# The order in which the PSUM banks go to the products behind the attention

## The chip, the cores and the metric

The kernel runs on one core of a Trainium2 chip. The metric is the device time of one execution in microseconds (us). TensorE (PE, with its weight loads as PEld) multiplies into PSUM, eight banks of 512 float32 values for each of 128 partitions; VectorE (DVE) and ScalarE (ACT) read and write PSUM and the on-chip memory SBUF; GpSimd (POOL) works on SBUF alone; SyncE (SP) issues most of the transfers. Each engine works through its own queue in order and waits on semaphores for the others.

## The reference

An attention over 2 batches of 12 heads (448 positions, 64 dimensions) is followed by two layers on its 896 x 768 output. The change concerns the first product of the first layer, h = x @ w_in.

```python
scores = scale * np.matmul(q, k.transpose(0, 1, 3, 2))        # causal mask, softmax -> attn
attn_out = np.matmul(attn, v)
x = attn_out.transpose(0, 2, 1, 3).reshape(B * S, H * D)      # 896 x 768

h = x @ w_in                                                  # 768 x 2048
g = np.where(h >= 1, h, np.where(h <= -1, 0.0, (h + 1) ** 2 / 4.0))
x = g @ w_out                                                 # 2048 x 768

gate, val = x @ w_gate, x @ w_val                             # 768 x 1536 each
out = (gate * (1.0 / (1.0 + np.exp(-gate))) * val) @ w_out2   # 1536 x 768
```

## The kernel before

Every product of the layers is made in three matmuls: each operand is split into a high part (what float32r keeps) and a low rest, and high x high, high x low and low x high are summed in PSUM (`mm3`, L85 to L88). x is kept transposed, in two groups g of 448 token columns: group 0 is the first half of the positions of both batches, group 1 the second half. h is made in 16 slices f of 128 rows; a product of a slice and a group is 6 x 3 = 18 matmuls of 128 x 448 into one bank (`h_products`, L267). Its squashing leaves the bank by several steps on DVE and ACT.

The attention runs first, group 0 and then group 1, as a software pipeline whose order is written out in `ORDER`. It holds seven of the eight banks: two score tiles of two banks (`ps_s`), one of two banks for the transposes (`ps_t`), one for the values (`ps_o`). One bank is left, the pool `mm_a` (L310). While group 1's attention runs, this bank takes the h products of group 0, slices 0 to 8, one after the other (`filler`, L488). Each is read by `h_relu` (L282) and `h_max` (L287, L288), and with L288 the bank is free for the next; `g_hi` and `g_lo` (L293, L297) then work on a copy in SBUF.

After the attention its seven banks go to a new pool `mm_b` (L564). The products that follow are group 1's slices 0 to 8 and then both groups' slices 9 to 15 (`h_chunk`, L567). Here a bank is read and written by five steps: L575 (DVE), L576 (ACT, on the clipped copy), L578 (DVE, back into the bank), L293 (ACT) and L297 (DVE); only then is it free. Between these steps `W.tick` puts the preparation of the weights to come: three operations of `narrow` on DVE (L99, L102, L105), a cast on ACT (L195) and a subtraction on POOL (L196).

Which bank a product gets is decided by `bank()` (L262): it takes the first pool of the list `banks`, puts it at the end and asks it for a tile. During the attention the list holds `mm_a` alone. A tile waits until the last user of its bank is done. A scheduler then arranges the instructions of each engine by the times that it estimates, so that products written one after the other can change places or interleave; in the order printed below, a number behind a tile's name tells tiles apart. Tiles 1748 and 1821 are the eighth and the ninth product in `mm_a`, 1860 the first and 1890 the second product of `h_chunk`.

Of the kernel before, what the change touches and what calls it, by code (L numbers as in the profile page):

```python
# [63 lines left out]
def fused_kernel(ctx: ExitStack, tc: tile.TileContext, qk, v, w_in, w_out, w_gv, w_o2, out):  # L64
# [195 lines left out]
    banks = []  # L260
# [301 lines left out]

    gt1 = gctx.enter_context(tc.tile_pool(name="gt1", bufs=1))
    mm_b = ctx.enter_context(tc.tile_pool(name="mm_b", bufs=7, space=PSUM))  # L564
    banks += [mm_b] * 7

    def h_chunk(g, f, gt):  # L567
        for ps in h_products(g, f):
# [246 lines left out]
```

## Time and profile before

| | |
|---|---|
| median of 3 runs | 603.63 us (603.3 to 603.74) |
| the profiled execution | 603.42 us |
| its span, first to last instruction | 601.6 us |
| TensorE busy | 593.4 us, 99% |
| VectorE busy | 441.5 us, 73% |
| ScalarE busy | 232.4 us, 39% |
| GpSimd busy | 117.1 us, 19% |

The profile page and the trace are of one execution; 603.42 - 601.6 = 1.8 us of its time lie outside the span. A busy time is an average over the whole program, so the stretches are read apart: the attention with its fillers up to about 146 us, the rest of h up to about 230 us, and then the second product of the first layer and the second layer. A matmul's row lasts longer than the distance to the next matmul's start, since matmuls are pipelined: what one costs in a row of them is the distance from start to start.

### The profile page before, as it was taken

How to read it: one execution, taken by the hardware profiler on the slowest of the kernel's cores; microseconds unless marked ns; L12 is line 12 of the kernel's file. 1: busy time of each engine (PE TensorE's matmuls, PEld its weight loads, DVE VectorE, ACT ScalarE, POOL GpSimd, SP SyncE). 2: the span in 40 equal slices, each digit the busy share in tenths (PEclk: the TensorE clock that was granted, in tenths of full speed). 3: DMA queues.
4: the chain of work that ended last, by engine and by line, in shares of the span. 5: the costliest groups of instructions: out<-in, count | busy, mean ns of one | idle time of the engine just before them, and what ended most of it. 6: DMA issues, size and time to landing. Idle time of an engine off the chain costs nothing.

```text
span 601.6 us, 8762 instructions
## 1 busy us (share of the span) xinstructions
PE 593.4 (99%) x3334; PEld 521.3 (87%) x3334; DVE 441.5 (73%) x811; ACT 232.4 (39%) x499; POOL 117.1 (19%) x68
## 2 busy tenths in 40 slices
PE   9999999999999999999999999999999999999997
PEld 5766667668999999999999999999999999999997
DVE  3999999872886777666874699489787899863401
ACT  3987777653344433111121454224224342512100
POOL 0000000000311221323133212124122233632300
PEclk9999999999999999999999999999999999999999
DMA  8575554300151234567644303133333333544002
GB/s 260 175 212 171 172 176 151 106 1 1 53 158 33 84 93 150 182 210 245 194 133 146 106 1 105 53 105 106 103 111 103 105 106 115 200 157 145 1 1 92
DMA packets 23417, 72.52 MB, mean 121 GB/s; under 512 B 2640, under 2 KB 9616, under 8 KB 23376
## 3 DMA queue, kind: packets, MB, share of 16 engines
q1 hardware_dynamic: 20784, 69.61, 36.7%
q10 hardware_dynamic: 2592, 2.36, 1.1%
q8 instruction: 26, 0.43, 0.3%
q14 instruction: 15, 0.12, 0.1%
HBM read 66.85 MB, written 5.11 MB: 120 GB/s over the span
## 4 chain that ended last, share of the span: by engine, by line
PE 84%; DVE 13%; ACT 1%; DMA 1%; issue 0%; ACTq 0%
PE mm L81 34%; PE mm L660 27%; PE mm L749 5%; PE mm L751 5%; PE mm L750 5%; DVE s L368 3%; DVE p L406 2%; PE mm L83 2%; PE s L81 1%; DVE wt L105 1%; DVE wt L102 1%; PE mm L473 1%; ACT p L382 1%; DVE wl L196 1%; DMA wraw<-w_in 1%; PE t L83 1%
## 5 line engine op out<-in xcount | busy, mean ns | idle before, releaser
L196 POOL TENSOR_TENSOR wl<-wt,wh 128x768 fp32r<-128x768 f32 (+1 forms) x52 | 102.5, 1976 | 428.3 <-ACT wh L195 428.3
L195 ACT CAST wh<-wt 128x768 fp32r<-128x768 f32 (+1 forms) x61 | 49.7, 816 | 152.0 <-DVE wt L105 40.7
L99 DVE TENSOR_SCALAR wt<-wraw 128x768 int32<-128x768 int32 (+1 forms) x64 | 44.9, 701 | 41.8 <-POOL wl L196 36.7
L102 DVE SCALAR_TENSOR_TENSOR wt<-wraw,wt 128x768 int32<-128x768 int32 (+1 forms) x64 | 72.5, 1132 | 0.8
L81 PE MATMUL mm<-gh,wh 128*128 128x448 f32 x192 | 70.1, 365 | 0.0
L81 PE MATMUL mm<-gh,wl 128*128 128x448 f32 x192 | 70.1, 365 | 0.0
L81 PE MATMUL mm<-gl,wh 128*128 128x448 f32 x192 | 70.1, 365 | 0.0
L660 PE MATMUL mm<-yl,wh 128*128 128x448 f32 x180 | 65.7, 365 | 0.0
L660 PE MATMUL mm<-yh,wl 128*128 128x448 f32 x180 | 65.7, 365 | 0.0
L660 PE MATMUL mm<-yh,wh 128*128 128x448 f32 x180 | 65.7, 365 | 0.0
L105 DVE SCALAR_TENSOR_TENSOR wt<-wraw,wt 128x768 int32<-128x768 int32 (+1 forms) x64 | 64.4, 1007 | 0.7
L81 PE MATMUL mm<-xh,wh 128*128 128x448 f32 x165 | 62.6, 379 | 2.4 <-DVE q L288 2.4
L749 PE MATMUL mm<-wh,uh 128*128 128x384 f32 x168 | 56.1, 334 | 0.0
L750 PE MATMUL mm<-wl,uh 128*128 128x384 f32 x168 | 56.1, 334 | 0.0
L751 PE MATMUL mm<-wh,ul 128*128 128x384 f32 x168 | 56.1, 334 | 0.0
L382 ACT ACTIVATE p<-s,mx 112x112 f32<-112x112 f32 (+3 forms) x96 | 46.4, 497 | 20.0 <-DVE mx L370 14.4
L81 PE MATMUL mm<-xl,wh 128*128 128x448 f32 x138 | 50.4, 365 | 0.0
L81 PE MATMUL mm<-xh,wl 128*128 128x448 f32 x138 | 50.2, 365 | 0.0
L368 DVE TENSOR_REDUCE s<-s 112x2 f32<-112x224 f32 (+3 forms) x48 | 35.4, 743 | 6.9 <-PE s L83 6.7
L81 PEld LDWEIGHTS mm<-gl,wh 128*128 128x128 f32 x192 | 36.1, 188 | 2.9
L81 PEld LDWEIGHTS mm<-gh,wl 128*128 128x128 f32 x192 | 36.1, 188 | 2.9
L81 PEld LDWEIGHTS mm<-gh,wh 128*128 128x128 f32 x192 | 36.1, 188 | 2.8
(132 smaller groups left out, 1216.8 us busy)
## 6 DMA issues: line engine op xcount, KB each, us to landing
wraw<-w_gv SPq DMA_DIRECT2D x18, 768.0 KB, 4.3
wraw<-w_in SPq DMA_DIRECT2D x16, 768.0 KB, 4.7
wraw<-w_out SPq DMA_DIRECT2D x12, 768.0 KB, 4.6
wraw<-w_o SPq DMA_DIRECT2D x12, 768.0 KB, 4.2
araw<-w_gv SPq DMA_DIRECT2D x18, 256.0 KB, 4.8
qk_t<-qk SPq DMA_DIRECT2D x12, 336.0 KB, 3.2
wraw<-w_out SPq DMA_DIRECT2D x6, 512.0 KB, 3.8
qk_t<-qk SPq DMA_DIRECT2D x12, 224.0 KB, 3.9
```

The source lines that it names most:

```text
L81: return product(*args, **kw)
L99: yield nc.vector.tensor_scalar(out=t, in0=w[:, :, 1], scalar1=3, scalar2=0x3FFFFFF8, op0=ALU.logical_shift_left, op1=ALU.bitwise_and,)
L102: yield nc.vector.scalar_tensor_tensor(out=t, in0=w[:, :, 1], scalar=-0x40000000, in1=t, op0=ALU.bitwise_and, op1=ALU.bitwise_or,)
L105: yield nc.vector.scalar_tensor_tensor(out=t, in0=w[:, :, 0], scalar=29, in1=t, op0=ALU.logical_shift_right, op1=ALU.bitwise_or,)
L195: nc.scalar.copy(out=wh[:, :n], in_=t)
L196: (nc.vector if i < LOW_V else nc.gpsimd).tensor_tensor(out=wl[:, :n], in0=t, in1=wh[:, :n].bitcast(F32), op=ALU.subtract,)
L368: nc.vector.tensor_reduce(out=mx[:, i], in_=s[:C, :, off:off + w], axis=AX.X, op=ALU.max)
L382: nc.scalar.activation(out=p[:, h, off:off + w], in_=s[:C, h, off:off + w], func=AF.Exp, bias=mx[:, i, h:h + 1], scale=0.125, accum_out=sm ...
L660: nc.tensor.matmul(out=ps[:, :N], lhsT=w[a][:, sl], rhs=rows[c][b], start=(first and c == i == 0), stop=(last and c == i == 2), skip_group ...
L749: nc.tensor.matmul(out=ps, lhsT=c, rhs=a, start=(f == 0), stop=False)
L750: nc.tensor.matmul(out=ps, lhsT=c, rhs=b, start=False, stop=False)
L751: nc.tensor.matmul(out=ps, lhsT=d, rhs=a, start=False, stop=(f == FC2 - 1))
```

## The change

The seven banks of `mm_b` are put in front of `mm_a` in the list, and no longer behind it.

```diff
     gt1 = gctx.enter_context(tc.tile_pool(name="gt1", bufs=1))
     mm_b = ctx.enter_context(tc.tile_pool(name="mm_b", bufs=7, space=PSUM))
-    banks += [mm_b] * 7
+    banks[:0] = [mm_b] * 7
```

Before, the first product of `h_chunk` gets the bank `mm_a`, the second to eighth get the banks of `mm_b`, and the ninth `mm_a` again. Now the first to seventh get the banks of `mm_b` and the eighth gets `mm_a`. The circle of eight banks stays the same for all that follows.

TensorE (PE) where the attention's last h product ends, before:

```order
L83 MATMUL mm_1821<-xh_74,wl_1702 128x448
L81 MATMUL mm_1890<-xh_76,wh_764 128x448 [waits DVE_49]
L81 MATMUL mm_1890<-xl_77,wh_764 128x448
...
L81 MATMUL mm_1860<-xh_76,wh_468 128x448 [waits DVE_49]
L81 MATMUL mm_1860<-xl_77,wh_468 128x448
...
L81 MATMUL mm_1860<-xh_76,wl_469 128x448
L81 MATMUL mm_1890<-xh_76,wl_765 128x448
```

The same place on TensorE after the change:

```order
L83 MATMUL mm_1821<-xh_74,wl_1702 128x448
L81 MATMUL mm_1860<-xh_76,wh_468 128x448 [waits DVE_49]
L81 MATMUL mm_1860<-xl_77,wh_468 128x448
...
L81 MATMUL mm_1860<-xh_76,wl_469 128x448
L81 MATMUL mm_1890<-xh_76,wh_764 128x448
L81 MATMUL mm_1890<-xl_77,wh_764 128x448
```

Before, 11 of the second product's 18 matmuls stand ahead of the first product and 7 behind it; now the two products stand one after the other, and the second has no wait of its own. Nothing else on PE moves.

VectorE (DVE) behind the attention's last h product, before (`gl1_0` and `gl1_1` are the low parts of the first and second product's result, `wt_2010` the twelfth weight, which L99 to L105 narrow):

```order
L575 TENSOR_SCALAR m_1879<-mm_1860 128x448 [waits PE_49]
L578 TENSOR_TENSOR mm_1860<-mm_1860,m_1879 128x448 [waits Activation_49]
L575 TENSOR_SCALAR m_1909<-mm_1890 128x448 [waits PE_49]
L99 TENSOR_SCALAR wt_2010<-wraw_1913 128x768 [waits DMAHW3_49,Pool_49]
L297 TENSOR_TENSOR gl1_0_1886<-mm_1860,gh1_0_1885 128x448 [waits DMAHW6_49,DMAHW4_49,DMAHW7_49,DMAHW1_49,Activation_49]
L578 TENSOR_TENSOR mm_1890<-mm_1890,m_1909 128x448 [waits Activation_49]
L102 SCALAR_TENSOR_TENSOR wt_2010<-wraw_1913,wt_2010 128x768 [waits DVE_49]
L297 TENSOR_TENSOR gl1_1_1917<-mm_1890,gh1_1_1916 128x448 [waits Activation_49]
```

The same place on VectorE after the change:

```order
L575 TENSOR_SCALAR m_1879<-mm_1860 128x448 [waits PE_49]
L578 TENSOR_TENSOR mm_1860<-mm_1860,m_1879 128x448 [waits Activation_49]
L99 TENSOR_SCALAR wt_2010<-wraw_1913 128x768 [waits DMAHW3_49,Pool_49]
L102 SCALAR_TENSOR_TENSOR wt_2010<-wraw_1913,wt_2010 128x768 [waits DVE_49]
L297 TENSOR_TENSOR gl1_0_1886<-mm_1860,gh1_0_1885 128x448 [waits DMAHW6_49,DMAHW4_49,DMAHW7_49,DMAHW1_49,Activation_49]
L575 TENSOR_SCALAR m_1909<-mm_1890 128x448 [waits PE_49]
L105 SCALAR_TENSOR_TENSOR wt_2010<-wraw_1913,wt_2010 128x768 [waits DVE_49]
L578 TENSOR_TENSOR mm_1890<-mm_1890,m_1909 128x448 [waits Activation_49]
```

The narrowing of the twelfth weight, L99 and L102, now stands ahead of the first step on the second product. Some 25 rows of DVE and nine of ACT change places in this way over the next five products; behind them the order is as before, and POOL and SP have the same instructions in the same order throughout.

## Rows read from the trace of the kernel before

**Rows 1.** The page: busy us, share of the span, instructions.

```profile
PE 593.4 (99%) x3334; PEld 521.3 (87%) x3334; DVE 441.5 (73%) x811; ACT 232.4 (39%) x499; POOL 117.1 (19%) x68
```

**Rows 2.** Busy time by stretch; columns in the first row.

```profile
core 0: us, PE busy (x) PEld busy (x) DVE busy (x) ACT busy (x) POOL busy (x), PEclk, DMA share, GB/s
0.00:141.90 141.90, 137.18 (x1013) 92.59 (x1013) 120.62 (x345) 98.18 (x279) 0.94 (x7) 1.00 0.49 151
141.90:598.19 456.29, 456.25 (x2322) 428.68 (x2322) 320.30 (x467) 134.19 (x221) 116.14 (x61) 1.00 0.35 112
598.19:601.60 3.41, 0.00 (x0) 0.00 (x0) 0.55 (x1) 0.00 (x0) 0.00 (x0) 1.00 0.15 58
```

**Rows 3.** Waits of PE, whole span; PEld, 138 to 200: total us, times, longest.

```profile
PE mm L81 <- DVE q L288: 2.4, 4, 1.3
PE mm L473 <- DVE half_b L478: 1.2, 1, 1.2
PE o L81 <- ACT pt L426: 0.9, 1, 0.9
PE s L81 <- ACT p L382: 0.2, 1, 0.2
...
PEld mm L81 <- DVE q L288: 1.0, 2, 0.8
```

**Rows 4.** Chain of waits around the ninth product's start: start us, us, what.

```profile
139.89 0.64 ACT r L282
...
140.56 0.64 DVE q L287
...
141.22 0.64 DVE q L288
...
141.90 0.47 PE mm L81
```

**Rows 5.** Timeline at the handover: start us, us, engine, line, operation, [idle before].

```profile
145.44 0.37 PE L83 MATMUL mm<-xh,wl 128*128 128x448 f32 x1
145.65 0.36 PE L81 MATMUL mm<-xh,wh 128*128 128x448 f32 x1
...
147.24 0.62 DVE L288 TENSOR_TENSOR q<-mm,q 128x448 f32<-128x448 f32 x1
...
147.68 0.36 PE L81 MATMUL mm<-xl,wh 128*128 128x448 f32 x1
...
147.92 0.19 PEld L81 LDWEIGHTS mm<-xh,wh 128*128 128x128 f32 x1 [0.26 <-DVE q L288]
147.92 0.47 PE L81 MATMUL mm<-xh,wh 128*128 128x448 f32 x1
...
148.23 0.37 PE L81 MATMUL mm<-xl,wh 128*128 128x448 f32 x1
```

**Rows 6.** Busy time of an undisturbed stretch, columns as in rows 2.

```profile
151.88:184.91 33.03, 33.03 (x164) 30.61 (x163) 28.77 (x40) 13.97 (x23) 7.35 (x4) 1.00 0.31 96
```

**Rows 7.** Timelines of POOL, DVE and PE behind the handover.

```profile
152.59 3.65 POOL L196 TENSOR_TENSOR wl<-wt,wh 128x768 fp32r<-128x768 f32 x2 [151.05 <-ACT wh L195]
...
154.48 2.18 DVE L99 TENSOR_SCALAR wt<-wraw 128x768 int32<-128x768 int32 x1
156.58 0.61 DVE L297 TENSOR_TENSOR gl<-mm,gh 128x448 fp32r<-128x448 f32 x1
...
157.65 0.94 DVE L102 SCALAR_TENSOR_TENSOR wt<-wraw,wt 128x768 int32<-128x768 int32 x1
...
161.00 0.55 DVE L99 TENSOR_SCALAR wt<-wraw 128x768 int32<-128x768 int32 x1
...
174.98 0.37 PE L81 MATMUL mm<-xh,wh 128*128 128x448 f32 x1
```

**Rows 8.** Groups by line, 142 to 199 us: count, busy us, mean ns, idle before.

```profile
L102 DVE SCALAR_TENSOR_TENSOR wt<-wraw,wt 128x768 int32<-128x768 int32 x6 | 8.1, 1348 | 0.1
...
L99 DVE TENSOR_SCALAR wt<-wraw 128x768 int32<-128x768 int32 x6 | 5.0, 826 | 1.6 <-POOL wl L196 1.5
```

## The prediction

> **What bounds the kernel now.** I read the page's busy times first. TensorE is busy 593.4 us of a span of 601.6 [rows 1], so the kernel is already almost one row of matmuls, and the question is only in which stretches it is not. The table by stretches answers that [rows 2]. Up to 141.90 us TensorE is busy 137.18 us of 141.90; from there to 598.19 us it is busy 456.25 of 456.29; then follows a tail of 3.41 us in which it does nothing. The granted clock is 1.00 in all three, which is the 2.4 GHz level, so no stretch is slow for that reason. The change takes effect where the attention hands over to the remaining h products, at about 145.65 us, so it falls into the middle stretch, where TensorE has 0.04 us of idle time in 456. Nothing can be taken out there but the work itself, or a bubble that the busy time hides because the row of the matmul ahead reaches into it.
>
> The list of TensorE's waits names the candidate: line 81 waited for the DVE operation q of line 288, 2.4 us in 4 waits, the longest 1.3 us [rows 3]. That is the attention's one bank: each h product must wait until L288 has read the product before it for the last time. It would be a mistake to book the 2.4 us to this change. The chain of waits shows where the last of them lies [rows 4]: the eighth product's matmuls end, then come L282, L287 and L288, and the ninth starts at 141.90 us. It belongs to the attention's own nine products, which the change leaves on the one bank; the wait at the handover is not among the four. It shows only in the list of the weight loads (PEld): 1.0 us in 2 waits, 0.8 of it the one at 141.90 [rows 3], which leaves 0.2 to 0.3 for the other.
>
> What the handover itself costs is seen in order of time [rows 5]. The ninth product's last matmul starts at 145.44; the next row starts at 145.65, one pitch later, without a wait, and by the order of the instructions it belongs to tile 1890 in the first of the seven new banks. The old bank becomes free when L288 ends, at 147.24 + 0.62 = 147.86 us. In between TensorE runs 11 matmuls of tile 1890, the last starting at 147.68, and the first on the old bank (tile 1860) starts at 147.92. So the scheduler has already put useful work under the wait, and what is left is the difference between 2.27 us (145.65 to 147.92) and 11 pitches.
>
> **The change part by part.**
>
> Pitch. In an undisturbed piece 164 matmuls start within 33.03 us, counting the first and the last [rows 6]; that is 33.03 / 163 = 0.2026 us from start to start.
>
> The bubble. From 147.68 to 148.23 there are two pitches, 0.405 us undisturbed, but 0.55 us in the rows [rows 5]. The bubble is 0.145 us. Its first piece is 147.68 to 147.92, 0.24 instead of 0.20: a gap of 0.04. The rest is 147.92 to 148.23, 0.31 instead of 0.20: the weights of the waiting matmul start loading at 147.92 together with it, where in other rows they load while the matmul before them runs. With the change, tile 1860 stands in the bank that tile 1890 had, which is free at 145.65 (the row of tile 1890 shows no wait there); tile 1890 takes the second new bank. Both old users of these banks, the attention's scores, ended long before; the last x_lo of the attention, on which every product of group 1 depends, is done too, since tile 1890 needs it too and did not wait. The old bank comes to the eighth product after the handover, 7 products of 18 matmuls later (25.5 us after 145.65), when it has been free for over 20 us. **Gain: 0.145 us.** The lower bound is 0, if the late load is paid again where the two products now meet; the upper bound is the bubble itself, since TensorE has no other idle time near. I take the upper end, since the nearest row of two products that meet on free banks, 145.44 to 145.65, goes on at the pitch.
>
> On the load the Trainium skill can be set against the row. In the page "TensorE: Matmul & The Clock Gate", section "Step-by-step: what each phase is for", it says that TensorE pulls a weight load ahead of matmuls in flight when it goes to the background weight buffer. By that the weights of the waiting matmul would have been in place before 147.92, only the 0.04 us would be bubble, and the sum would come to 603.38 us; the row, where the load starts only at 147.92, after 0.26 us of idle time, speaks for the 0.145.
>
> What moves on the other engines. On PE 11 matmuls move behind 18; none is added or removed. The first product of group 1 is therefore complete 11 matmuls (2.2 us) earlier and the second at the same place as before. DVE and ACT take up the first product's five steps (L575, L576, L578, L293, L297) earlier; on DVE the narrowing of the next weight (L99, L102) now stands ahead of L575 of the second product. Both queues are in order, so if L99 waits for GpSimd, all that stands behind it waits: L297 of the first product and the whole chain of the second. L99 did not wait here before, but it was slow: 2.18 us at 154.48, beside a GpSimd row that runs from 152.59 for 3.65 us, against 0.55 us at 161.00 [rows 7]. Such a stretch is worth 1.6 us, on DVE. Its cover is the bank turn: the first product's bank was released at 156.58 + 0.61 = 157.19 us and is asked for again by the product that starts at 174.98 us [rows 7], so 17.8 us are free. From 142 to 199 us six L102 had a mean of 1.35 us against 0.94 for one that ran beside no GpSimd row, and six L99 had 0.83 against 0.55 [rows 7, 8]: 6 x 0.41 + 6 x 0.28 = 4.1 us of stretching in all. Even doubled it does not use up 17.8 us. **Cost: 0**, under that cover.
>
> The weights. The slot that the tenth weight is cast into (L195) comes free when the first product of group 1 has been through, some 2 us earlier than now; it was not late before, since none of TensorE's waits is for a weight [rows 3]. Nothing is gained. SP and POOL issue the same instructions in the same order, so no transfer moves past another.
>
> The rotation. There are eight banks in the same circle before and after, only entered one place later, so every later tile follows the last user of its bank by eight tiles as before. The tail is untouched: TensorE ends at 598.19 us [rows 2], and the last copy and the output transfer follow.
>
> Sum against the profiled execution: 603.42 - 0.145 = 603.28 us. That execution lies 0.21 us below the median of the three runs, 603.63; from the median the same step gives 603.49. I put the forecast between, at **603.4 us**. The gain is 0.02%, a tenth of the 0.2% (1.2 us) that a measurement of this kernel can tell from no change, and less than the 0.44 us between the three runs.
>
> **Rivals.**
>
> A: the whole wait comes back as gain. If the handover had cost what the old bank's wait lasts, 2.27 us, the time would be 603.42 - 2.27 = 601.15 us, faster by 0.4%. For it speaks that the wait is real: L282, L287 and L288 take 1.9 us after the ninth product. Against it speak the 11 matmuls in the rows between 145.65 and 147.68; they are work that must be done anyway, and after the change it is done later. Chance 0.02.
>
> B: the reordered DVE queue makes TensorE wait (slower). The place is the ninth product after the handover, at 174.98 us, the first that reuses a bank: if DVE hangs on L99 behind GpSimd so long that the first product's bank is not released by then, TensorE stands until the release has run. The nearest row for such a stand is the attention's own, from L282 at 139.89 to the ninth product at 141.90 [rows 4]: 2.01 us, which gives 603.28 + 2.01 = 605.3 us, slower by 0.3%. It decides from a delay of 17.8 us on. For it speaks that the order moves L99 and L102 forward, and that they collide with GpSimd; against it, that the stretch of the whole window is 4.1 us. Chance 0.03.
>
> C: the bubble stays. If the change only swaps which product pays for a late weight load, the time is 603.42 us from the profiled run and 603.63 from the median. For it speaks that two products still meet at 145.65 and at 149.3; against it, the pitch from 145.44 to 145.65. Chance 0.12, on the same side of every bound as the forecast.
>
> **How the numbers follow.** Forecast 0.83, A 0.02, B 0.03, C 0.12. Faster by over 0.2% needs A: 0.02. Slower by over 0.2% needs B: 0.03. Within 0.2%: 0.95. For the range the unknown costs give hardly any width, 603.28 to 603.63. What remains is the run itself: the stretch up to 141.90 us, with its waits for transfers and its queues on DVE, is where runs can differ, and three runs spread over 0.44 us. I allow twice that on either side, 602.5 to 604.3 us.
>
> **What would show it.** In the profile of the changed kernel: the weight loads' waits for q of L288 fall from two to the one at 141.90, while TensorE's own four stay; from 145.65 on all matmuls start 0.20 us apart, with none that is 0.47 us long; the first product's 18th matmul starts near 145.65 + 17 x 0.2026 = 149.1 us, and L575 follows at once; and the stretch from the ninth product's start to TensorE's end shrinks from 456.29 us by 0.1 to 0.2. The prediction is wrong if a gap on PE appears near 175 us (B), if TensorE waits for a weight between 178 and 210 us, or if that stretch shrinks by more than 0.5 us (A).

## The result: 610.9 us, 1.2% slower

The changed kernel takes 610.91 us (median of 4 runs, 610.19 to 611.10) against 603.68 us of the kernel before in the same measurement (4 runs, 603.30 to 603.85). The ratio is 1.0119, its 95% interval 1.0101 to 1.0136. The forecast was 603.4, no change. The time lies outside the range, on the side that had a chance of 0.03, and the mechanism given for that side is not what happened.

First the busy times of the profile after, one row for all engines (compare [rows 1]), and the two stretches in which TensorE works, with the columns of [rows 2]:

```profile
PE 600.1 (99%) x3334; PEld 521.1 (86%) x3334; DVE 434.7 (71%) x811; ACT 232.7 (38%) x499; POOL 114.6 (19%) x68
```

```profile
0.00:141.57 141.57, 136.79 (x1012) 92.54 (x1012) 120.56 (x345) 98.02 (x279) 0.94 (x7) 1.00 0.48 151
141.57:604.98 463.41, 463.35 (x2322) 428.53 (x2322) 313.58 (x467) 134.65 (x221) 113.68 (x61) 1.00 0.34 110
```

The span grew from 601.6 to 608.4 us, and TensorE's busy time grew by as much with it: 600.1 instead of 593.4 us for the same 3,334 matmuls. The stretch up to the ninth product is 0.33 us shorter, the tail behind it takes 3.42 us (3.41 before), and the stretch between them went from 456.29 to 463.41 us: 7.12 us, with 0.06 us of idle time and a granted clock of 1.00, the 2.4 GHz level, as before. Nothing waits longer. The list of TensorE's waits, and that of the weight loads from 138 to 200 us (total us, times, longest), against [rows 3]:

```profile
PE mm L81 <- DVE q L288: 2.3, 4, 1.3
...
PEld mm L81 <- DVE q L288: 0.8, 1, 0.8
```

The second wait of the weight loads, that of the handover, is gone. The timeline of TensorE at the handover shows the same, against [rows 5]:

```profile
145.39 0.37 PE L81 MATMUL mm<-xh,wh 128*128 128x448 f32 x1
...
147.87 0.37 PE L81 MATMUL mm<-xh,wh 128*128 128x448 f32 x1
148.07 0.37 PE L81 MATMUL mm<-xl,wh 128*128 128x448 f32 x1
```

The row runs through without the matmul of 0.47 us. So the change does what it was meant to do, and the loss is in no gap. It is seen in the count of matmuls in a stretch of 100 us; columns as in [rows 2]. First 200 to 300 us after the change, then the same of the kernel before:

```profile
200.00:300.00 100.00, 100.00 (x486) 90.81 (x485) 69.21 (x123) 24.87 (x40) 23.99 (x14) 1.00 0.52 167
```

```profile
200.00:300.00 100.00, 100.00 (x495) 92.67 (x494) 71.62 (x123) 24.70 (x41) 24.13 (x14) 1.00 0.52 168
```

There are 486 matmuls where there were 495, in a stretch without any idle time: every matmul costs 1.9% more. Where this begins and ends is seen in the chain of waits after the change (start us, us, what):

```profile
141.57 0.47 PE mm L81
142.04 1.03 PE mm L83 x5
...
145.55 204.60 PE mm L81 x990
...
517.55 0.18 PE mm L749
```

990 matmuls in 204.60 us are 206.67 ns from start to start, where [rows 6] gave 202.6. It holds from the ninth product on (1.03 us for five matmuls, where before it was 1.01) to 517.55 us, where the last stage begins, whose matmuls have 384 columns (L749). The kernel before begins that stage at 510.76 us. From the ninth product's start it takes 375.98 us to get there, before 368.86: all of the 7.12 us. The last stage takes 87.43 us in both (517.55 to 604.98, 510.76 to 598.19). 375.98 us at 206.67 ns are 1,819 matmuls; 1,819 x 4.0 ns = 7.28 us, less the bubble that went.

So 448-column matmuls have two steady paces, 202.67 and 206.67 ns from start to start. What sets them was the question for the chip. Single executions of one and the same kernel fall into two groups, near 603.6 and near 610.6 us; a run below that has no trace is counted as fast or slow by its time.

### The profile page after: what moved, and what is told of

The parts are those of the page before. It is cut to its first block, busy times and chain, and to the rows that moved or that the text cites. A ratio compares the mean times of both kernels' runs of the same rounds, so it can differ in the third digit from the quotient of the medians.

```text
span 608.4 us, 8761 instructions
## 1 busy us (share of the span) xinstructions
PE 600.1 (99%) x3334; PEld 521.1 (86%) x3334; DVE 434.7 (71%) x811; ACT 232.7 (38%) x499; POOL 114.6 (19%) x68
## 4 chain that ended last, share of the span: by engine, by line
PE 83%; DVE 13%; DMA 2%; ACT 1%; issue 0%; SPq 0%; ACTq 0%
PE mm L81 34%; PE mm L660 28%; PE mm L750 5%; PE mm L751 5%; PE mm L749 5%; DVE s L368 3%; DVE p L406 2%; PE mm L83 2%; DVE wt L105 1%; PE s L81 1%; DVE wt L102 1%; ACT p L382 1%; DVE wl L196 1%; DMA wraw<-w_in 1%; PE t L83 1%; PE s L83 1%
## 5 line engine op out<-in xcount | busy, mean ns | idle before, releaser
L196 POOL TENSOR_TENSOR wl<-wt,wh 128x768 fp32r<-128x768 f32 (+1 forms) x52 | 100.3, 1931 | 436.2 <-ACT wh L195 436.2
L99 DVE TENSOR_SCALAR wt<-wraw 128x768 int32<-128x768 int32 (+1 forms) x64 | 40.1, 627 | 47.9 <-POOL wl L196 46.4
L81 PE MATMUL mm<-gh,wh 128*128 128x448 f32 x192 | 70.7, 368 | 0.0
L81 PE MATMUL mm<-gl,wh 128*128 128x448 f32 x192 | 70.7, 368 | 0.0
L81 PE MATMUL mm<-gh,wl 128*128 128x448 f32 x192 | 70.7, 368 | 0.0
L102 DVE SCALAR_TENSOR_TENSOR wt<-wraw,wt 128x768 int32<-128x768 int32 (+1 forms) x64 | 68.5, 1071 | 0.9
L105 DVE SCALAR_TENSOR_TENSOR wt<-wraw,wt 128x768 int32<-128x768 int32 (+1 forms) x64 | 65.2, 1019 | 0.7
L81 PE MATMUL mm<-xh,wh 128*128 128x448 f32 x165 | 62.9, 381 | 2.3 <-DVE q L288 2.3
L749 PE MATMUL mm<-wh,uh 128*128 128x384 f32 x168 | 56.1, 334 | 0.0
L81 PE MATMUL mm<-xl,wh 128*128 128x448 f32 x138 | 50.8, 368 | 0.0
L81 PE MATMUL mm<-xh,wl 128*128 128x448 f32 x138 | 50.8, 368 | 0.0
L81 PEld LDWEIGHTS mm<-gh,wh 128*128 128x128 f32 x192 | 36.0, 188 | 3.7
L81 PEld LDWEIGHTS mm<-gl,wh 128*128 128x128 f32 x192 | 36.0, 188 | 3.6
L81 PEld LDWEIGHTS mm<-gh,wl 128*128 128x128 f32 x192 | 36.0, 188 | 3.6
```

Source lines behind the costliest of these rows:

```text
L81: return product(*args, **kw)
L99: yield nc.vector.tensor_scalar(out=t, in0=w[:, :, 1], scalar1=3, scalar2=0x3FFFFFF8, op0=ALU.logical_shift_left, op1=ALU.bitwise_and,)
L102: yield nc.vector.scalar_tensor_tensor(out=t, in0=w[:, :, 1], scalar=-0x40000000, in1=t, op0=ALU.bitwise_and, op1=ALU.bitwise_or,)
L105: yield nc.vector.scalar_tensor_tensor(out=t, in0=w[:, :, 0], scalar=29, in1=t, op0=ALU.logical_shift_right, op1=ALU.bitwise_or,)
L196: (nc.vector if i < LOW_V else nc.gpsimd).tensor_tensor(out=wl[:, :n], in0=t, in1=wh[:, :n].bitcast(F32), op=ALU.subtract,)
L749: nc.tensor.matmul(out=ps, lhsT=c, rhs=a, start=(f == 0), stop=False)
```

## Experiments

The letters in the expectations stand for these theories. P: the pace is taken where a row of matmuls starts anew, and kept until something interrupts the row. L: it differs from execution to execution of one program. B: the bank that the products get, or their order, sets it. V: an old bank that comes early in the circle protects against the slow pace. Three more came later: D, each new start is a draw whose odds hang on its timing; W and W2, the width of the matmuls ahead of a row sets its pace. In the two runs on the handover's restart, W has another meaning: the short wait sets the pace anew.

**The same two kernels again.** No edit.

> The changed kernel once more. Its trace has no new wait; every 448-column matmul from the ninth product on starts 206.7 ns after the one ahead, where the kernel before has 202.7 on average, over about 1,780 matmuls (4.0 ns x 1,780 = 7.1 us). Theory P (pace): a row of matmuls takes one of two steady paces, fixed by how the row starts after an idle gap, and keeps it until the next gap; the changed kernel has no gap after the ninth product's start. If the start falls the same way every time: 610 to 611 us in every run, 206.7 ns in the trace. Theory L (lottery): each run draws anew, so single runs lie either near 603.5 or near 611. Theory B (bank): the place of the products in the banks sets the pace; 610 to 611 us in every run as well.

> The kernel before once more, for its trace. Theory P (pace drawn where a row of matmuls starts): the ninth product may have either pace (202.7 or 206.7 ns), but from the restart at the handover, the matmul that waits some 0.04 us for the old bank, the pace is 202.7 ns, since all runs of this kernel so far lie between 602.5 and 604.9 us. If the ninth product's pace simply carried through the handover, a ninth product at 206.7 ns would give 206.7 ns behind it and 611 us.

The changed kernel gave 603.41, 603.73 and 603.86 in three runs and 610.17 to 611.57 in seven. The profile is of the run of 603.73: first a stretch with the columns of [rows 2], then the chain.

```profile
200.00:300.00 100.00, 100.00 (x495) 92.68 (x495) 70.91 (x123) 25.54 (x41) 25.54 (x15) 1.00 0.53 173
```

```profile
142.36 0.47 PE mm L81
142.83 1.01 PE mm L83 x5
...
511.07 0.18 PE mm L749
```

The same program, the fast pace from the ninth product on: the pace is not fixed by the instructions (L). With this B falls too, as far as it gives a program one pace. From the ninth product to the 384-column stage it takes 368.71 us, against 368.86 before: 0.15 us less. That is the gain of 0.145 us that the prediction worked out, visible as soon as the pace is the same. The kernel before gave 603.54 here. In the comparisons with the other kernels it ran 81 times; 80 of these runs lie between 602.56 and 605.54 us and one at 610.98. Going by its time, that one run was at the slow pace: the kernel before can fall into it too, but hardly ever does. The changed kernel did so in 11 of 14 runs.

**The old bank second.** Against the changed kernel:

```diff
-    banks[:0] = [mm_b] * 7
+    banks[:] = [mm_b] + banks + [mm_b] * 6
```

> The old bank is handed out second: the first product behind the attention takes the first new bank, the second takes the old one, which is free by then. The instructions stand in exactly the changed kernel's order and there is no gap at the handover. Theory P: as the changed kernel, 610 to 611 us, pace 206.7 ns (or, with another draw at the ninth product's start, 603.5). Theory B: only six of the first eight products are where the changed kernel has them, so a pace of its own for some products, 604 to 610 us. If the gap at the handover were what costs time, 603.3.

603.20 and 603.76 in two runs, 609.72 to 612.74 in eight; ratio to the kernel before 1.0105, 1.0078 to 1.0133. The instructions are in the order of the changed kernel, only the banks differ, and the odds (eight slow in ten) are near those of the changed kernel. So the bank of the first product doesn't set the pace, and V falls.

**One additional matmul ahead of every other product.** Against the changed kernel; the additional matmuls' result is overwritten by the product.

```diff
+    extra = []
...
         ps = bank()
+        if extra:
+            n = extra.pop(0)
+            if n:
+                nc.tensor.matmul(out=ps[:, :n], lhsT=wh[:, :128], rhs=xh[:, 0, :n], start=True, stop=True)
...
     banks[:0] = [mm_b] * 7
+    for n in (32, 64, 96, 128, 160, 192, 224, 256, 320, 352, 384, 416):
+        extra += [n, 0]
```

> The changed kernel, with one extra matmul of 32 to 416 columns (12 widths) ahead of every other product behind the attention, in the same bank; the product's own first matmul overwrites it. The row of matmuls is not interrupted, only shifted by a matmul of another width. Theory P: the pace of the 448-column matmuls may change at an extra matmul and at nothing else, so stretches of 36 matmuls have 202.7 or 206.7 ns; the extra work itself costs 1 to 3 us. Theory B: the pace stays 206.7 ns throughout, since banks and order are the changed kernel's. Theory L: one pace for the whole row.

611.2 us. The chain around the last additional matmul (L277, 416 columns):

```profile
220.92 7.30 PE mm L81 x36
228.22 0.19 PE mm L277
228.41 71.70 PE mm L81 x347
```

Ahead of it 36 matmuls take 7.30 us, 202.8 ns each; behind it 347 take 71.70, 206.6 ns. The eleven other widths passed without a change of pace. So the pace can change in the middle of a row, at one matmul of another width and without a gap, and it then stays for the rest of the row. This agrees with P, which expected a change at an additional matmul and nowhere else.

**Pauses.** Against the changed kernel: at every third product TensorE waits for a copy that DVE makes out of the product before.

```diff
+    gaps, before = [], []
...
         ps = bank()
+        if gaps and gaps.pop(0):
+            z = ev.tile([128, 128], BF16, tag="z", name="z")
+            follow(nc.vector.tensor_copy, False, out=z, in_=before[0][:, :128])
+            follow(nc.tensor.matmul, False, out=ps[:, :128], lhsT=z, rhs=z, start=True, stop=True)
+        before[:] = [ps]
...
+    gaps += [0, 1, 0] * 7
```

> The changed kernel, with a 128-column matmul ahead of every third product that waits for a DVE copy out of the product before, so that TensorE pauses for some 0.5 to 1 us at up to seven places; the product overwrites what it wrote. Theory P: each pause lets the pace be drawn again, so the stretches between pauses have 202.7 or 206.7 ns, and the last pause fixes the pace of the rest; 604 to 607 us if it falls to 202.7, about 612 to 615 if to 206.7. Theory B: 206.7 ns throughout and 612 to 615 us.

639.76 us, far above the expected 604 to 615, as the pauses came out at 1.2 to 7.1 us instead of 0.5 to 1: 24.5 us are waiting, and behind each of the four long pauses 10 to 14 distances are 0.37 us long (granted clock 0.88 from 146 to 258 us). A wait of the list (total us, times, longest), two rows of the timeline, and a stretch:

```profile
PE mm L83 <- DVE z L83: 24.5, 5, 7.1
```

```profile
201.00 0.37 PE L81 MATMUL mm<-xh,wh 128*128 128x448 f32 x1
...
203.90 0.37 PE L81 MATMUL mm<-xh,wl 128*128 128x448 f32 x1
```

```profile
300.00:400.00 100.00, 100.00 (x495) 92.69 (x494) 68.48 (x105) 28.42 (x42) 24.90 (x15) 1.00 0.40 130
```

Here the ninth product ran at the slow pace, the pieces behind the pauses at the fast one except that from 200.6 to 204 us (14 distances from 201.00 to 203.90, 207 ns each), and the long row behind the last pause at the fast one (495 in 100 us). Behind a pause either pace can follow, whatever the one ahead of it was.

**One additional matmul ahead of the second product.** The edit of the run with twelve widths, with `extra += [0, 32]` and `extra += [0, 192]`.

> The changed kernel with one extra matmul of 32 columns ahead of the second product behind the attention, and no gap. Theory P: an extra matmul of another width starts the pace anew as a gap does, so the share of slow runs need not be that of the changed kernel (about 4 in 5); single runs lie near 603.5 or near 611, the 0.1 us of the extra work apart. If only a real pause can change the pace: the changed kernel's share, about 8 of 10 near 611.

> As the kernel with the extra 32 columns, with 192 columns. Theory P: single runs near 603.5 or near 611 again, with a share that depends on the width; if only a pause can change the pace, about 8 of 10 near 611.

With 32 columns seven runs of 603.44 to 605.38 and three of 610.90 to 611.95; with 192 columns eight of 603.01 to 604.05 and two of 610.63 and 612.60. The profiled execution with 32 columns shows the change of pace itself:

```profile
145.02 1.03 PE mm L83 x5
146.05 3.72 PE mm L81 x18
149.77 0.02 PE mm L277
149.79 150.26 PE mm L81 x741
```

18 matmuls at 206.7 ns, then the additional one, then 741 at 202.8. The order, the banks and all other instructions are those of the changed kernel, and one matmul turned odds of 3 in 14 for the fast pace into 15 in 20. So the loss is in the pace that the row gets, and a new start behind the ninth product changes its odds. These 20 runs were on another chip than the ten of the changed kernel above; one matmul of 512 columns (below) ran on the same chip as those ten and was fast in 7 of 10, against 3 of 10.

**The kernel before without its cover.** The scheduler must keep the first two products in order, so that TensorE waits for the old bank.

```diff
-        for ps in h_products(g, f):
+        kept = (g, f) in ((1, 0), (1, 1))
+        for ps in h_products(g, f, ((False, False), (False, False)) if kept else ((True, True), (True, True))):
```

> The kernel before, with the first two products behind the attention held in program order on PE: the first waits for the old bank with nothing ahead of it, so TensorE pauses from about 145.65 to 147.9 us. It measures the wait that the 11 matmuls cover: 2.1 to 2.3 us, so 605.8 us where the pace behind it is 202.7 ns, and about 613 where it is 206.7. Theory P: either, in shares set by how the row starts out of a full pause, as at the ninth product of the changed kernel (about 4 in 5 slow). If the old bank in the first place is what protects the kernel before: 605.8 in all runs.

Four runs of 607.01 to 608.48, two of 613.63 and 614.19. The profile is of the last one: the timeline of TensorE at the pause ([idle before]), and two stretches.

```profile
147.76 0.67 PE L83 MATMUL mm<-xh,wh 128*128 128x448 f32 x1 [2.10 <-DVE q L288]
148.23 0.58 PE L83 MATMUL mm<-xl,wh 128*128 128x448 f32 x1
...
151.22 0.41 PE L83 MATMUL mm<-xh,wh 128*128 128x448 f32 x1
```

```profile
149.00:153.00 4.00, 4.00 (x16) 3.62 (x15) 0.00 (x0) 0.00 (x0) 0.00 (x0) 0.71 0.00 0
200.00:300.00 100.00, 100.00 (x485) 90.81 (x485) 68.74 (x121) 25.78 (x41) 24.76 (x15) 1.00 0.48 156
```

Two things are in it. The uncovered wait costs about 4 us (607 to 608.5 against 603.6): the pause of 2.1 us, and behind it eight distances of 0.37 us from 148.23 to 151.22, at a granted clock of 0.71 between 149 and 153 us, which is partly the 1.2 GHz level. And a pause of 2.1 us on the old bank does not see to the fast pace: two in six runs are slow. V forecast 605.8 us in all six.

**The handover's restart, moved.** In the kernel before, a matmul of 32 columns ahead of the 11 covering matmuls (the same edit, `extra += [0, 32]`); and, in another kernel, the old bank released later by a DVE copy of 128 columns:

```diff
         nc.vector.tensor_tensor(out=q, in0=ps[:, :N], in1=q, op=ALU.max)
+        if f == EARLY - 1:
+            late = ev.tile([128, 128], F32, tag="late", name="late", bufs=1)
+            nc.vector.tensor_copy(out=late, in_=ps[:, :128])
```

> The kernel before with one extra matmul of 32 columns ahead of the 11 that cover the wait for the old bank. The chain that ends the wait (the ninth product's end, L282, L287, L288) keeps its place; TensorE's row of 11 is shifted by some 0.1 us, so the gap at the handover shrinks from 0.04 us to nothing or nearly so. Theory W (the wait is what sets the pace anew, and without it the ninth product's pace, possibly changed by the extra matmul, carries on): some of ten runs near 611, as with the extra 32 columns in the changed kernel (3 of 10), the others near 603.6. Rival V (the old bank in the first place protects, wait or not): all runs near 603.6.

> The kernel before, with one more DVE copy of 128 columns out of the old bank behind the ninth product's L288, so that the bank comes free about 0.25 us later; the scheduler puts a twelfth matmul ahead of the waiting one, so a short wait remains, of another length and at another place. Theory W: a short wait sets the pace anew; if every such restart falls to 202.7 ns, all runs lie at 603.5 to 604; if a restart is a draw, some lie near 611, and the kernel before owes its constancy to the exact length of its chain. Rival V: all runs near 603.6.

With the additional matmul eight runs of 603.38 to 604.37 and two of 610.34 and 610.65. The gap did not shrink, as it was expected to: the scheduler left ten matmuls of the second product ahead of the waiting one instead of 11, and that one starts 0.34 us behind the last of them, where in the kernel before it is 0.24. So this run moves the restart and does not take it away. With the late release five of 603.15 to 603.83 and five of 610.29 to 611.20. Its weight loads show that the short wait of the handover is still there, only with another releaser:

```profile
PEld mm L81 <- DVE late L291: 0.2, 1, 0.2
```

There the waiting matmul starts 0.23 us behind the one ahead, nearly as in the kernel before. A short wait as such is therefore not what protects the kernel before. Its restart looks like a draw whose odds hang on the place: where it stands the fast pace comes out in 80 of 81 runs, and one matmul and some 0.2 us later in five of ten. V, which forecast 603.6 for all runs, fails in both kernels. This agrees with D; whether the time counts or the number of matmuls ahead is not separated.

**Seven widths in turn.** In the kernel before, rows of 24 additional matmuls ahead of 21 products.

```diff
+    extra = []
...
+        if extra:
+            n = extra.pop(0)
+            for i in range(24 if n else 0):
+                nc.tensor.matmul(
+                    out=ps[:, :n], lhsT=(wh, wh, wl)[i % 3][:, i // 3 % KC * 128:][:, :128],
+                    rhs=(xh, xl, xh)[i % 3].rearrange("p c n -> p (c n)")[:, i // 3 % 5 * N:][:, :n],
+                    start=True, stop=True,
+                )
...
+    extra += [0, 0] + [512, 480, 464, 432, 416, 384, 320] * 3
```

> The kernel before, with 24 extra matmuls of one width ahead of each of 21 products behind the attention (512, 480, 464, 432, 416, 384 and 320 columns, three times each), overwritten by the product. It measures the pace of each width, with the same change of weights at each matmul. Theory P says nothing on which widths have two paces; in the traces so far 384 columns have 173.3 ns alone and 448 have 202.7 or 206.7. The extra work is about 504 x 0.2 = 100 us: some 700 us.

The chain, second round of the widths (L277 are the additional matmuls, L81 the product behind each):

```profile
211.82 5.46 PE mm L277 x24
217.27 3.65 PE mm L81 x18
220.92 5.20 PE mm L277 x24
...
229.76 5.03 PE mm L277 x24
...
238.44 4.70 PE mm L277 x24
243.14 3.71 PE mm L81 x18
246.84 4.53 PE mm L277 x24
251.37 3.71 PE mm L81 x18
255.08 4.17 PE mm L277 x24
259.25 3.71 PE mm L81 x18
262.96 3.52 PE mm L277 x24
```

The seven other widths took the same time in each of their three rows, to 0.01 us; only 448 shows two paces. The 18 matmuls of a product take 3.65 us (202.8 ns) behind 512, 480, 464 and 320 columns and 3.71 (206.1) behind 432, 416 and 384, in all three rounds. This looks like a rule, that the width ahead sets the pace (W), so it was tried in both directions.

**The rule of the widths, tried.** Such a row of 24 ahead of one product: 416 columns in the kernel before, 512 in the changed one, and one single matmul of 512 in the changed one. The edit is that of the run with seven widths, with the number of matmuls beside the width; the last line is that of 416 columns, and in the changed kernel it is `extra += [(0, 0), (512, 24)]` and `extra += [(0, 0), (512, 1)]`.

```diff
-            n = extra.pop(0)
-            for i in range(24 if n else 0):
+            n, times = extra.pop(0)
+            for i in range(times):
...
+    extra += [(0, 0)] * 2 + [(416, 24)]
```

> The kernel before with 24 additional matmuls of 416 columns (discarded work, into the third product's bank ahead of it) behind the handover, about 153 us. They cost 24 x 0.188 = 4.5 us themselves. Theory W (the width of the matmuls ahead sets the pace at which the 448-column row goes on: after 416 columns it was 206.7 ns in three of three places): every run in the slow group, 603.6 + 4.5 + about 1,720 x 0.0040 = 615.0 us; in the profile 202.7 ns from the handover to the additional matmuls and 206.7 behind them to about 517 us. Theory D (each shift is a draw whatever the width): a mixture of runs near 608.1 and near 615.0. Theory B (only the bank's place in the circle matters, which is that of before): all runs near 608.1 us.

> The changed kernel with 24 additional matmuls of 512 columns (discarded work) ahead of its second product, about 149.3 us. They cost 24 x 0.2267 = 5.4 us. Theory W (after 512 columns the row went on at 202.7 ns in three of three places, from either pace): every run near 603.6 + 5.4 = 609.0 us, whatever pace the ninth and first product have (a difference of 0.15 us at most). Theory D: a mixture of runs near 609.0 and 616.0 us. If the change itself, by the bank it gives the first product, made the row slow: all near 616.0.

> The changed kernel with one additional matmul of 512 columns (discarded work) ahead of its second product. It costs 0.23 us. Theory W, if one matmul is enough: every run 603.5 to 604.2 us. If it takes a row of them, or theory D: a mixture of runs near 603.7 and near 610.4 us, as one matmul of 32 columns (7 of 10 fast) and one of 192 (8 of 10) gave.

416 columns: 608.28 to 608.71 in all four runs, not one slow. W falls: its forecast was 615.0. (It is what B forecast, but B had fallen with the first experiment; D left it open how many would be slow.) 512 columns: 609.11 to 609.75 in all four runs. This agrees with W but also with D: at the 15 in 20 of other additional matmuls, four of four would come out in a third of all cases. A single one of 512 columns: seven runs of 603.47 to 604.13, three of 611.22 to 611.56; the mixture of D, and no repair of the change.

**The remaining form of the rule.** In the run with seven widths the pace went to slow only behind 432 and to fast only behind 320, and could have been kept by the others (W2). In the kernel before, 24 of 432 columns ahead of the third product; and the same with 24 of 320 columns nine products later.

```diff
+    extra += [(0, 0)] * 2 + [(432, 24)] + [(0, 0)] * 8 + [(320, 24)]
```

> The kernel before with 24 additional matmuls of 432 columns (discarded work) ahead of its third product behind the attention; they cost 24 x 0.1959 = 4.7 us. In the run with rows of several widths the pace went from 202.7 to 206.7 ns behind the 432-column rows (three of three) and back behind the 320-column rows (three of three), and was kept behind 416, 384, 512, 480 and 464. Theory W2 (certain widths change the pace, the others keep it): every run 603.7 + 4.7 + about 1,720 x 0.0040 = 615.3 us, with 206.7 ns behind the additional matmuls. Theory D (each start is a draw with odds that hang on its timing; the three repeats were alike because they were placed alike): runs near 608.4 us, or a mixture of 608.4 and 615.3.

> The same with, nine products later, 24 additional matmuls of 320 columns (discarded work), 24 x 0.1467 = 3.5 us. Theory W2: 206.7 ns between the two rows and 202.7 ns behind the second, so every run 603.7 + 4.7 + 3.5 + 9 x 18 x 0.0040 = 612.6 us. Theory D: runs near 611.9 (never slow), near 612.6, or up to 618.9 us (slow behind the second row).

608.17 us (607.57 to 608.85, four runs) and 612.11 us (611.39 to 612.34, four runs). W2 wanted 615.3 for the first. Its profiled execution refutes W2 in place (L276 are the additional matmuls); first the timeline at the handover, then the chain:

```profile
145.64 0.37 PE L81 MATMUL mm<-xh,wh 128*128 128x448 f32 x1
...
146.67 0.37 PE L81 MATMUL mm<-xh,wl 128*128 128x448 f32 x1
...
147.91 0.46 PE L81 MATMUL mm<-xh,wh 128*128 128x448 f32 x1
148.21 0.36 PE L81 MATMUL mm<-xl,wh 128*128 128x448 f32 x1
...
149.22 0.36 PE L81 MATMUL mm<-xh,wh 128*128 128x448 f32 x1
```

```profile
153.24 4.70 PE mm L276 x24
157.94 193.34 PE mm L81 x954
```

Behind the 432 columns 954 matmuls run at 202.66 ns. In the second kernel the nine products between its two rows, in the chain:

```profile
158.44 32.83 PE mm L81 x162
```

That is 202.65 ns again; 603.7 + 4.7 + 3.5 = 611.9 us is near its median. So neither 416 nor 432 columns give a slow pace to what follows, and the repeats of the run with seven widths were probably alike because what stood ahead of them was alike. All 16 timed runs with one or two rows of 24 are fast, 12 of them in the kernel before, which is nearly always fast; so the odds of single additional matmuls (22 of 30 fast) need not hold for every start.

The timeline shows one more thing. The ninth product and the 11 covering matmuls ran at the slow pace here too (five distances take 1.03 us from 145.64), and behind the handover the pace is the fast one (1.01 from 148.21). In the run with seven widths it is the same. All six traces in which the handover is that of the kernel before are fast behind it, and in these two it was slow ahead of it. So in the kernel before, this restart decides, and not the ninth product. And the matmul on the old bank does not even start late here: it starts 0.20 us behind the one at 147.71. What is left of the bubble is the distance behind it, 0.30 instead of 0.20. A restart needs no gap.

## Why the prediction was wrong

**What bounds the kernel.** Right: TensorE is the bound, and nothing could be gained beyond the bubble. "Nothing can be taken out there but the work itself" was true; that something could be added to the work itself, without a wait, was not thought of.

**Pitch.** This step failed. It took 202.6 ns out of one undisturbed piece and used it as a constant of the matmul. It is one of two values, 202.67 and 206.67. The sum used it for two matmuls and the 11 of the cover, while the change decides at the handover for the 1,801 behind the ninth product; 4.0 ns each are 7.2 us, fifty times the bubble. That rows can go at more than one pace stood in the trace of before, had it been read to the nanosecond. Between the attention's other work lie pieces of five matmuls; the timeline of two of them, first and last row each:

```profile
133.23 0.36 PE L83 MATMUL mm<-xl,wh 128*128 128x448 f32 x1
...
134.05 0.37 PE L83 MATMUL mm<-xh,wl 128*128 128x448 f32 x1
...
138.68 0.36 PE L83 MATMUL mm<-xl,wh 128*128 128x448 f32 x1
...
139.49 0.37 PE L83 MATMUL mm<-xh,wl 128*128 128x448 f32 x1
```

Four distances take 0.82 us in the one and 0.81 in the other, the same work at the same granted clock. These hundredths alone can't tell: four distances in the fast row behind the handover come out at 0.81 or 0.82 too. The nanoseconds in the trace can: 201, 207, 206 and 207 in the first piece, the beginning of the slow pace, and 196, 199, 206 and 203 in the second. A hundredth looks like rounding; over 1,800 matmuls it is the result.

**The bubble.** Right, and in its size: 0.145 us forecast, 0.15 measured in the traced run of the changed kernel that had the fast pace (368.71 against 368.86 us). The upper end of its bound was the right choice: the late weight load went with the wait, and it was not 0.04 us alone. But the wait of 0.04 us with its late weight load was not only a cost. It interrupted the row, and with that it gave the row behind it a new start, which at this place came out fast in 80 of 81 runs. Without it the ninth product's pace goes on (slow in the first trace of the changed kernel, fast in the second), and by their times it was slow in 11 of 14 runs. A step that removes a wait must ask what the wait resets.

**What moves on the other engines.** Cost 0 was right, even on the good side. Groups by line on DVE from 142 to 199 us, against [rows 8]:

```profile
L105 DVE SCALAR_TENSOR_TENSOR wt<-wraw,wt 128x768 int32<-128x768 int32 x5 | 7.1, 1412 | 0.0
L102 DVE SCALAR_TENSOR_TENSOR wt<-wraw,wt 128x768 int32<-128x768 int32 x6 | 5.7, 954 | 0.1
```

The stretch of 4.1 us that was doubled for safety moved and got smaller. L102 and L99 now run when GpSimd's subtraction has ended (954 ns, and 552 where it was 826), but L105, which had 946 ns (mean of five) before, now runs beside it in part and takes 1412: five times 0.47 us are 2.3 us. The run of the changed kernel at the fast pace has the same (955, 553 and 1399 ns), so it belongs to the order. It brings nothing to the time, as DVE has room. Weights and the rotation: no wait of TensorE for either, as forecast.

**Rivals.** A (the whole wait back) did not come: the 11 matmuls were real cover. Without them the wait costs about 4 us, more than the 2.27 of rival A, as the granted clock is lower behind the pause (0.71). B (DVE makes TensorE wait at 174.98 us) did not come: there is no gap. C stayed on the side of the forecast; the bubble did go. None of the rivals had to do with the length of the matmuls' own row.

**The range.** It was made from three runs of one kernel that nearly always has the same pace, and their spread of 0.44 us was put down to the stretch before 141.90 us. The chance of 0.95 for no change took that spread for what a run can do. A second program with another start was outside of what three runs could show.

**What would show it.** The weight loads' waits for q of L288 fell from two to one, no matmul behind 145.39 is 0.47 us long, and the first product's 18th matmul starts at 148.90 us, near the 149.1 that was written. "All matmuls start 0.20 us apart" is where the profile said no: 0.21, and the stretch grew by 7.12 us instead of shrinking by 0.1 to 0.2.

**What stays open.** Why a start brings one pace or the other. It is not the bank of the first product, not the width ahead by itself, and not whether there is a short wait. The runs agree with odds that hang on the timing of the start, but none shows it, and what in TensorE keeps the two paces apart no row shows. The ninth product's own odds are open too: in the 18 traces, whose work is the same up to there, it is slow in 7, while by their times 19 of 24 runs of the changed kernel and of the one with the old bank second are slow. Nor is there a version that beats the kernel before: it has the fast pace in nearly every run, and the changed kernel with 192 columns ahead of its second product has a median of 603.44 us, ratio 1.0009 (0.9983 to 1.0035), with two runs in ten 7 us and more above it.

## What to carry to other kernels

In a kernel that is one long row of matmuls, the distance from start to start is a term of its own: count matmuls in a stretch without idle time, before and after, ahead of looking for waits. A wait of a few hundredths of a us in such a row can be worth keeping, since it restarts the row, and an edit that removes it can change the pace of everything up to the next interruption. One profile of one run shows one draw: repeat the timing of both kernels until the groups of runs can be seen, and compare runs of the same group.

## What the runs showed of the hardware

- Matmuls of 448 columns with a weight load each have two steady paces at a granted clock of 1.00: 204.60 us / 990 = 206.67 ns and 193.34 us / 954 = 202.66 ns. In the trace's nanoseconds the slow one repeats 206, 207, 207 and the fast one 199, 207, 203, 202, 203 (kernel after and kernel before, behind the ninth product's start). A pace was kept for up to 1,819 matmuls.
- By the chain of the run with seven widths, for 24 matmuls each: 512 columns 227 ns, 480 217, 464 210, 432 196, 416 189, 384 174, 320 147, with the same time in the three rows of each.
- The Trainium skill, page "TensorE: Matmul & The Clock Gate", section "Back-to-back issue gap", gives the isolated spacing at full clock as the columns over 2.4 GHz plus 2.5 ns; worked out for 448 columns that is an estimate of 189.2 ns. Both paces here lie above it, by 13.5 and by 17.5 ns, so the measurement decides.
- A pause of 2.1 us on TensorE was followed by eight distances of 0.37 us between matmuls, with a granted clock of 0.71 from 149 to 153 us, partly the 1.2 GHz level.
- VectorE's L105 (128 x 768, int32) took 1412 ns in the mean of five where three of them ran partly beside a GpSimd subtraction, and 946 where none did.
